# Attention and maxout FFN on one core: twin PSUM tiles in the prologue, other slots for the steps, and 30 of 40 transposes moved from TensorE to the DMA crossbar

## Chip, cores, metric

The kernel runs on one core of a Trainium2 chip. The metric is the device time of one execution in microseconds; lower is better. A "fast" run is one within 1.5% of the fastest run of the same kernel, and verdicts use fast runs alone.

## The reference

Eight batches of eight heads, 576 tokens, head size 64. Keys and values are averaged over groups of eight tokens, so attention goes over 72 pooled positions. The result, 4608 tokens by 512, passes through a maxout FFN.

```python
k_p = k.reshape(B, H, Sp, 8, D).mean(axis=3)         # Sp = 72
v_p = v.reshape(B, H, Sp, 8, D).mean(axis=3)
attn = softmax(q @ k_p.transpose / sqrt(D))
x = (attn @ v_p).transpose(0, 2, 1, 3).reshape(B * S, H * D)
h = maximum(maximum(x @ w1, x @ w2), x @ w3)         # 512 -> 768
out = h @ w_out                                      # 768 -> 512
```

## The kernel before

The FFN works in nine blocks of 512 tokens, and the attention of the next batch (576 tokens) is cut into steps that are emitted in chosen "slots" between the FFN's parts. The parts that matter here:

```python
def turn_x(b, c0, keep, xn, tag):          # 128 tokens of attention output, turned to [channel, token]
    pxt = psp.tile([128, KCH, 128], F16, name="pxt", ...)
    for kc in range(KCH):                  # KCH = 4
        nc.tensor.transpose(pxt[:, kc, :], xn[...], identh)
    nc.scalar.copy(out=xT[:, :, g0 + keep:g0 + 128], in_=pxt[:, :, keep:128])

def values(b, c0):                         # 8 matmuls into pav, then on DVE:
    ...
    xn = sb3.tile([128, 2, 4, D], F16, name="xn", tag="xn")     # sb3: three buffers
    nc.vector.tensor_tensor(out=xn, in0=pv[:, :, :, 0:D], in1=rcp..., op=ALU.mult)

CHUNKS = ((0, 0), (128, 0), (256, 0), (384, 0), (448, 64))      # five turns per batch

def hidden_part(n, jc, c0, c1, hT):        # three weights: 4 matmuls each on xT, ACT cast, DVE max, DVE max
    ...
def project(n, hT):
    for mm in range(4):
        # 6 matmuls into po
        osb = sb3.tile([128, C], F32, name="osb", tag="osb", bufs=5)
        nc.scalar.copy(out=osb, in_=po)
        for u in range(2):
            nc.sync.dma_start(out=dst[...], in_=osb[64 * u:64 * u + 64, :])    # 128 KB each
        yield

for n in range(1, TOK // NB):
    if n + 2 < B:
        fold_k(n + 2, nc.gpsimd); load_k(n + 3, nc.gpsimd)      # 1152 KB
        fold_v(n + 2); load_v(n + 3, nc.gpsimd); load_q(n + 3)  # 1152 and 576 KB
    # (the loads only where n + 3 < B)
    nxt = batch(n + 1)
    for part in (hidden(n, hT), project(n, hT)):
        for _ in part:
            # next(nxt) as often as PLAN names this slot
```

PE is TensorE, DVE is VectorE, ACT is ScalarE and POOL is GpSimd. `xn` is one chunk of attention output (128 tokens in rows), `xT` the input of the FFN with channels in rows; bringing the one into the other is called a turn. `et` are the exponentials, `kz` the keys as the scores need them, `pw`, `po` and the other p-names are tiles in PSUM. The landing of a transfer is counted from its issue.

The softmax here doesn't subtract the row's maximum and nothing guards it: scores larger than these inputs give would overflow.

Of the kernel before, what the change touches and what calls it, by code (L numbers as in the profile page):

```python
# [14 lines left out]
def kernel(  # L15
# [11 lines left out]
    nc = tc.nc  # L27
    dt = mybir.dt
    F32, BF16, F16 = dt.float32, dt.bfloat16, dt.float16

    B, H, S, D = q.shape
    POOL = 8
    Sp = S // POOL
# [12 lines left out]
    JCH = DFF // 128  # L46
# [8 lines left out]
    psp = ctx.enter_context(tc.tile_pool(name="psp", bufs=1, space=PSUM))  # L55
    ctx.enter_context(tc.manual_schedule())

    kts, vts, qbs, kps, qTs, ets = {}, {}, {}, {}, {}, {}
# [45 lines left out]
    identh = const.tile([128, 128], F16, name="identh", tag="identh")  # L104
# [39 lines left out]
    def pool_v(b, h, g, tag, evac):  # L144

        pvp = psp.tile([128, g - h, D], F32, name="pvp", tag=tag[0], bufs=tag[1])
        for j in range(POOL):
            nc.tensor.matmul(pvp, identh[0:Sp, :], vts[b][:, h:g, j, :],  # L148
                             start=(j == 0), stop=(j == POOL - 1))
        evac(out=vp_all[:, b, h:g, 0:D], in_=pvp[0:Sp])  # L150

    def turn_q(b, n0, n1, evac, tag):
        if b not in qTs:
            qTs[b] = sb2.tile([128, 2 * NG, 128], BF16, name="qT", tag="qT")
        pqt = psp.tile([128, n1 - n0, 128], BF16, name="pqt", tag=tag[0],
                       bufs=tag[1])
        qf = qbs[b].rearrange("p hp t d -> p (hp t d)")
        for n in range(n0, n1):
            nc.tensor.transpose(pqt[:, n - n0, :], qf[:, 128 * n:128 * n + 128],  # L159
                                ident)  # L160
        evac(out=qTs[b][:, n0:n1, :], in_=pqt)  # L161

    def turn_k(b, evacs, tag):
        pkt = psp.tile([128, 6, 96], BF16, name="pkt", tag=tag[0], bufs=tag[1])
        for i in range(6):
            nc.tensor.transpose(pkt[:, i, :], kps[b][:, i, :, :], ident[0:96, 0:96])
        for par in range(2):
            rows = slice(64 * par, 64 * par + 64)
            evacs[par](  # L169
                out=kz_all[b % 2][rows, par, :, 0:Sp].rearrange(  # L170
                    "p h (r i) -> p h r i", i=6),
                in_=pkt[rows].rearrange("p i (h r) -> p h r i", h=H))

    def pool_k(b, tag):

# [26 lines left out]
        score(b, h, psc[:, 512:576], 1, 3, 4)  # L202
        exp(ets[b][:, h, :], psc[0:Sp, 0:S])

    def turn_x(b, c0, keep, xn, tag):
        pxt = psp.tile([128, KCH, 128], F16, name="pxt", tag=tag[0], bufs=tag[1])
        for kc in range(KCH):
            nc.tensor.transpose(  # L208
                pxt[:, kc, :],
                xn[:, kc // 2, 2 * (kc % 2):2 * (kc % 2) + 2, :], identh)  # L210
        g0 = S * b + c0
        nc.scalar.copy(out=xT[:, :, g0 + keep:g0 + 128], in_=pxt[:, :, keep:128])  # L212

    def values(b, c0):
        pav = psp.tile([128, 2, 512], F32, name="pav", tag="att", bufs=2)
# [14 lines left out]
    CHUNKS = ((0, 0), (128, 0), (256, 0), (384, 0), (448, 64))  # L230
    TR = ("tr", 1)
    PW = ("pw", 3)
    V_V = (nc.vector.tensor_copy, nc.vector.tensor_copy)

    def queries(b):

        new_et(b)
        for m, (n0, n1) in enumerate(((0, 5), (5, 10), (10, 14), (14, 18))):
            turn_q(b, n0, n1, nc.scalar.copy, TR)
            yield  # L240
            if m == 2 and b > 1:
                turn_k(b, V_V, TR)
                yield
        for h in range(H):
            scores(b, h)
            yield

    def outputs(b, tags=(TR,) * 5):

        last = None  # L250
        for (c0, keep), tag in zip(CHUNKS, tags):
            xn = values(b, c0)
            yield
            if last:
                turn_x(*last)
                yield
            last = (b, c0, keep, xn, tag)
        turn_x(*last)
        yield
# [22 lines left out]
    def hidden(n, hT):  # L282

        halves = n < 2
        if halves:
            for c0 in (0, NB // 2):
                for jc in range(2):
                    yield from hidden_part(n, jc, c0, c0 + NB // 2, hT)
        for jc in range(2 if halves else 0, JCH):
            yield from hidden_part(n, jc, 0, NB, hT)  # L290

    def project(n, hT):
# [15 lines left out]
    def new_hT():  # L308
        return sb2.tile([128, JCH, NB], F16, name="hT", tag="hT")
# [4 lines left out]
    def heat(n):  # L314
        for _ in range(n):
            nc.tensor.matmul(wm, warm[:, 0:128], warm, start=True, stop=True)  # L316

    new_et(0)
    heat(14)
    new_kp(0)  # L320
    k16 = const.tile([96, 6, 4, D], F16, name="k16", tag="k16")
    pkp0 = psp.tile([128, 6, D], F32, name="pkp", tag="pw", bufs=3)

    def spread(i0, i1):
        nc.vector.tensor_copy(out=kps[0][:, i0:i1, 0, :], in_=pkp0[0:96, i0:i1])
        nc.scalar.copy(out=kps[0][:, i0:i1, 1, :], in_=pkp0[0:96, i0:i1])

    for i in (0, 2, 4):
        c = slice(i, i + 2)
        nc.vector.tensor_tensor(out=k16[:, c], in0=kts[0][:, c, 0:4],  # L330
                                in1=kts[0][:, c, 4:8], op=ALU.add)
        for j in range(4):
            nc.tensor.matmul(pkp0[:, c], identh[0:96, :], k16[:, c, j, :],
                             start=(j == 0), stop=(j == 3))
        if i == 2:
            spread(0, 4)
        else:
            heat(1)
    spread(4, 6)
    heat(2)  # L340
    turn_k(0, (nc.vector.tensor_copy, nc.scalar.copy), PW)
    turn_q(0, 0, 5, nc.scalar.copy, PW)
    turn_q(0, 5, 9, nc.vector.tensor_copy, PW)

    def scores4(h):
        psc = psp.tile([128, 4, 256], F32, name="psc4", tag="att", bufs=2)
        for i in range(4):
            score(0, h + i, psc[:, i, :], 0, 0, 4)
        exp(ets[0][:, h:h + 4, 0:256], psc[0:Sp])

    def scores2(h):
        psc = psp.tile([128, 2, 512], F32, name="psc2", tag="att", bufs=2)
        for i in range(2):
            score(0, h + i, psc[:, i, 0:64], 0, 4, 5)
            score(0, h + i, psc[:, i, 64:320], 1, 0, 4)
        exp(ets[0][:, h:h + 2, 256:S], psc[0:Sp, :, 0:320])

    scores4(0)
    turn_q(0, 9, 14, nc.vector.tensor_copy, PW)
    turn_q(0, 14, 18, nc.vector.tensor_copy, PW)  # L360
    heat(1)
    scores4(4)
    scores2(0)
    pool_v(0, 0, 4, PW, nc.vector.tensor_copy)
    scores2(2)
    pool_v(0, 4, 6, PW, nc.vector.tensor_copy)
    scores2(4)
    pool_v(0, 6, 8, PW, nc.vector.tensor_copy)
    scores2(6)
    out0 = outputs(0, (PW, PW, TR, TR, TR))  # L370
    next(out0)
    heat(1)
    next(out0)
    heat(2)
    next(out0)
    heat(2)
    next(out0)
    next(out0)


    nc.vector.memset(kz_all[1], 0.0)
    hT0 = new_hT()
    def early():
        pool_k(1, TR)
        yield
        turn_k(1, V_V, TR)
        yield
        yield from queries(1)

    side = early()  # L390
    steps = {16: 1, 17: 1, 19: 1, 20: 1, 21: 1, 22: 1, 23: 2}
    for slot, _ in enumerate(hidden(0, hT0)):
        if slot < 5:
            next(out0, None)
        for _ in range(steps.get(slot, 0)):
            next(side)
    next(side)
    pool_v(1, 0, 4, TR, nc.scalar.copy)
    next(side)
    next(side)  # L400
    pool_v(1, 4, 8, TR, nc.scalar.copy)
    for _ in side:
        pass
    side = outputs(1)
    for _ in project(0, hT0):
        next(side)
        next(side)
    fold_k(2, nc.gpsimd)
    load_k(3, nc.gpsimd)
    load_q(3)  # L410
# [4 lines left out]
    def batch(b):  # L415
# [1 line left out]
        yield from outputs(b)  # L417


    PLAN = (1, 2, 4, 5, 7, 8, 9, 10, 11, 12, 13, 14, 15, 16, 17, 17, 18, 18, 19, 19,  # L420
            20, 20, 21)
    PLAN1 = (7, 8, 10, 13, 14, 15, 16, 17, 18, 19, 20, 21, 22, 23, 24, 24, 25, 25, 26,
             26, 27, 27, 27)
    for n in range(1, TOK // NB):
        if n + 2 < B:
            fold_k(n + 2, nc.gpsimd)
            if n + 3 < B:
                load_k(n + 3, nc.gpsimd)
            fold_v(n + 2)
            if n + 3 < B:  # L430
                load_v(n + 3, nc.gpsimd)
                load_q(n + 3)
        hT = new_hT()
        nxt = batch(n + 1) if n + 1 < B else iter(())
        plan = PLAN1 if n == 1 else PLAN
        slot = 0
        for part in (hidden(n, hT), project(n, hT)):
            for _ in part:
                if slot in (0, 2):
                    next(side, None)  # L440
                for _ in range(plan.count(slot)):
                    next(nxt, None)
                slot += 1
        for _ in nxt:
            pass


# [28 lines left out]
```

## Time and profile before

| | |
|---|---|
| time, median of 4 runs | 269.28 us |
| TensorE busy | 250.4 of 267.3 us (94%) |
| first FFN matmul | 20.83 us |
| first FFN matmul of block 2 | 84.21 us |
| a block with attention beside it / without | 27.36 / 20.72 us |

The prediction shows the busy table, the chain and TensorE's timeline. Two more rows: the granted TensorE clock and the busy share of the DMA engines, each in tenths for 40 slices of the span, and the line of DMA packets.

```profile
PEclk9999999999999999999999999999999999999998
DMA  7999999698757958969777604200330033006006
...
DMA packets 20866, 34.71 MB, mean 130 GB/s; under 512 B 2636, under 2 KB 13260, under 8 KB 20268
```

The clock is full throughout. The DMA engines are half busy or more until about 150 us, mostly with loads for later batches. TensorE waits for none of them.

### The profile page before, as it was taken

The page shows a single profiled execution, that of the slowest core. Times are in us where ns is not written, and L with a number is a line of the kernel's source. Part 1 is how long each engine was busy: PE and PEld are TensorE (multiplying, and loading weights), DVE is VectorE, ACT ScalarE, POOL GpSimd, SP SyncE. Part 2 cuts the span into 40 slices and gives each one's busy share as a digit, 9 for nine tenths or more (in the row PEclk, how much of TensorE's full clock was granted, in tenths as well). Part 3 has the DMA queues.
Part 4 walks back from the last instruction along what each step waited for, and adds up shares of the span by engine and source line. Part 5 has one row for each costly group of instructions (what it writes and reads, how often), then busy time and mean ns, then how long its engine had stood idle before and what let it go on. Part 6 is the DMA issues. An engine that isn't in the chain of part 4 may idle for free.

```text
span 267.3 us, 4638 instructions
## 1 busy us (share of the span) xinstructions
PE 250.4 (94%) x1858; PEld 139.6 (52%) x1860; DVE 128.1 (48%) x227; ACT 132.9 (50%) x232; POOL 117.7 (44%) x84
## 2 busy tenths in 40 slices
PE   7598998998998999999999999999999999999993
PEld 2477546574555455545555555545554554444441
DVE  3447562555453646363645464455536464433440
ACT  1374248553755474547465655465555653223221
POOL 8662002999899999859970895000000000000000
PEclk9999999999999999999999999999999999999998
DMA  7999999698757958969777604200330033006006
GB/s 188 201 198 205 202 244 211 168 245 180 178 121 180 285 126 184 256 202 174 178 156 221 94 0 105 54 0 2 85 76 0 0 81 79 0 22 139 0 2 156
DMA packets 20866, 34.71 MB, mean 130 GB/s; under 512 B 2636, under 2 KB 13260, under 8 KB 20268
## 3 DMA queue, kind: packets, MB, share of 16 engines
q0 software_dynamic: 14048, 21.44, 41.1%
q1 hardware_dynamic: 6796, 12.98, 19.3%
q8 instruction: 14, 0.23, 0.4%
q14 instruction: 8, 0.07, 0.1%
HBM read 34.60 MB, written 9.44 MB: 165 GB/s over the span
## 4 chain that ended last, share of the span: by engine, by line
PE 83%; DVE 9%; ACT 5%; issue 1%; DVEq 0%; ACTq 0%
PE pw L267 45%; PE po L297 17%; PE psc L188 6%; PE pxt L208 4%; PE pqt L159 3%; DVE kz L169 3%; PE pav L217 3%; PE wm L316 3%; ACT et L193 2%; DVE xn L225 2%; DVE t L275 2%; ACT t L272 1%; PE pvp L148 1%; DVE hT L278 1%; ACT qT L161 1%
## 5 line engine op out<-in xcount | busy, mean ns | idle before, releaser
L267 PE MATMUL pw<-xT,mw 128*128 128x512 f16 (+1 forms) x696 | 157.2, 364 | 0.9 <-ACT xT L212 0.7
L267 PEld LDWEIGHTS <-mw 128*128 128x128 f16 x696 | 62.2, 98 | 50.9 <-issue 1.2
L275 DVE TENSOR_TENSOR t<-t,pw 128x512 f16<-128x512 f16 (+1 forms) x58 | 37.8, 651 | 79.0 <-PE pw L267 48.4
L272 ACT CAST t<-pw 128x512 f16<-128x512 f32 (+1 forms) x58 | 32.3, 557 | 43.2 <-PE pw L267 42.6
L297 PE MATMUL po<-mwo,hT 128*128 128x512 f16 x216 | 51.5, 379 | 0.0
L193 ACT ACTIVATE et<-psc 72x576 f16<-72x576 f32 (+2 forms) x62 | 40.5, 662 | 13.0 <-PE psc L188 12.9
L278 DVE TENSOR_TENSOR hT<-t,pw 128x512 f16<-128x512 f16 (+1 forms) x58 | 37.7, 650 | 15.4 <-PE pw L267 13.4
L127 POOL TENSOR_TENSOR vt<-vt 72x2048 f32<-72x2048 f32 (+1 forms) x12 | 41.2, 3434 | 2.6 <-DMA vt<-in_v_dram 2.1
L127 POOL TENSOR_TENSOR kt<-kt 96x1536 f32<-96x1536 f32 (+1 forms) x12 | 31.5, 2624 | 22.7 <-DMA kt<-in_k_dram 22.1
L301 ACT COPY osb<-po 128x512 f32<-128x512 f32 x36 | 21.1, 586 | 30.5 <-PE po L297 30.5
L297 PEld LDWEIGHTS <-hT 128*128 128x128 f16 x216 | 19.8, 98 | 18.9 <-DVE hT L278 0.4
L212 ACT COPY xT<-pxt 128x512 f16<-128x512 f16 (+1 forms) x40 | 21.8, 545 | 14.3 <-PE pxt L208 14.3
L225 DVE TENSOR_TENSOR xn<-pav,rcp 128x512 f16<-128x512 f32 x40 | 27.7, 692 | 1.4
L188 PE MATMUL psc<-qT,kz 128*128 128x64 bf16 (+3 forms) x192 | 25.4, 246 | 3.1 <-ACT qT L161 1.7
L161 ACT COPY qT<-pqt 128x640 bf16<-128x640 bf16 (+1 forms) x29 | 18.6, 641 | 18.1 <-PE pqt L159 18.1
L188 PEld LDWEIGHTS <-kz 128*128 128x128 bf16 x192 | 18.1, 98 | 17.5 <-issue 2.9
L217 PEld LDWEIGHTS <-et 72*128 72x128 f16 x320 | 15.7, 98 | 8.2 <-issue 0.6
L223 DVE RECIPROCAL rcp<-pav 128x8 f32<-128x8 f32 x40 | 8.1, 204 | 23.1 <-PE pav L217 23.1
L208 PE MATMUL pxt<-identh,xn 128*128 128x128 f16 x160 | 15.5, 219 | 2.3 <-DVE xn L225 2.1
L217 PE MATMUL pav<-vp,et 72*128 72x65 f16 x320 | 17.1, 194 | 0.4 <-ACT et L193 0.3
L159 PEld LDWEIGHTS <-qb 128*128 128x128 bf16 x144 | 9.9, 97 | 11.4 <-DVE kz L169 5.3
L159 PE MATMUL pqt<-ident,qb 128*128 128x128 bf16 x144 | 13.0, 219 | 2.7 <-DVE kz L169 2.3
(41 smaller groups left out, 107.9 us busy)
## 6 DMA issues: line engine op xcount, KB each, us to landing
out_dram<-osb SPq DMA_DIRECT2D x72, 128.0 KB, 2.4
kt<-in_k_dram POOLq DMA_DIRECT2D x5, 1152.0 KB, 7.6
vt<-in_v_dram POOLq DMA_DIRECT2D x5, 1152.0 KB, 10.2
qb<-in_q_dram POOLq DMA_DIRECT2D x7, 576.0 KB, 11.8
mw<-in_moe_w_dram POOLq DMA_DIRECT2D x9, 256.0 KB, 9.7
kt<-in_k_dram SPq DMA_DIRECT2D x3, 384.0 KB, 5.1
kt<-in_k_dram SPq DMA_DIRECT2D x1, 1152.0 KB, 9.5
vt<-in_v_dram SPq DMA_DIRECT2D x1, 1152.0 KB
```

The source lines that it names most:

```text
L127: e.tensor_tensor(out=t[:, :, 0:n, :], in0=t[:, :, 0:n, :], in1=t[:, :, n:2 * n, :], op=ALU.add)
L159: nc.tensor.transpose(pqt[:, n - n0, :], qf[:, 128 * n:128 * n + 128], ident)
L188: nc.tensor.matmul(out, kz_all[b % 2][:, f % 2, h, :], qTs[b][:, n + i0:n + i1, 64 * (h % 2):64 * (h % 2) + 64], start=True, stop=True)
L193: nc.scalar.activation(out=out, in_=in_, func=FT.Exp, scale=1.0 / 64.0)
L208: nc.tensor.transpose(pxt[:, kc, :], xn[:, kc // 2, 2 * (kc % 2):2 * (kc % 2) + 2, :], identh)
L217: nc.tensor.matmul(pav[:, h // 4, 65 * (h % 4):65 * (h % 4) + 65], ets[b][:, h, c0:c0 + 128], vp_all[:, b, h, :], start=True, stop=True)
L225: nc.vector.tensor_tensor(out=xn, in0=pv[:, :, :, 0:D], in1=rcp.to_broadcast([128, 2, 4, D]), op=ALU.mult)
L267: nc.tensor.matmul(pw, w_sb[wi][:, kc, bass.ts(jc, 128)], xT[:, kc, col], start=(kc == 0), stop=(kc == KCH - 1))
L272: nc.scalar.copy(out=t, in_=pw)
L275: nc.vector.tensor_tensor(out=t1, in0=t, in1=pw, op=ALU.max)
L278: nc.vector.tensor_tensor(out=hT[:, jc, c0:c1], in0=t, in1=pw, op=ALU.max)
L297: nc.tensor.matmul(po, hT[:, jc, bass.ts(mm, 128)], wo_sb[:, jc, :], start=(jc == 0), stop=(jc == JCH - 1))
```

## The change

The intent is to take work off TensorE, the bound. In the prologue, two copies of a PSUM tile let DVE and ACT read at once, and the first chunks' values come earlier. Steps move to other slots, and the first two blocks work in half blocks for longer. For batches 2 to 7 the turn of the attention output becomes a DMA transpose on the sync queue, from xn in SBUF straight to xT, without PSUM and without the ACT copy.

```diff
+    def turn_x(b, c0, keep, xn, tag, evac=nc.scalar.copy):
+        if b > 1:
+            g0 = S * b + c0
+            nc.sync.dma_start_transpose(
+                out=xT[:, :, g0 + keep:g0 + 128],
+                in_=xn.rearrange("p g h d -> p (g h d)")[keep:128])
+            return
...
-    pkp0 = psp.tile([128, 6, D], F32, name="pkp", tag="pw", bufs=3)
+    pkp0 = [psp.tile([128, 6, D], F32, name="pkp", tag="pw", bufs=3)
+            for _ in range(2)]
...
+    pkt0 = [keys(0, PW) for _ in range(2)]
+    for h in (0, 4):
+        fill_kz(0, 0, h, h + 4, pkt0[0], nc.vector.tensor_copy)
+        fill_kz(0, 1, h, h + 4, pkt0[1], nc.scalar.copy)
...
-                for jc in range(2):
+                for jc in range(3):
...
-    PLAN = (1, 2, 4, 5, 7, 8, 9, 10, 11, 12, 13, 14, 15, 16, 17, 17, 18, 18, 19, 19,
-            20, 20, 21)
+    PLAN = (2, 4, 5, 6, 8, 8, 9, 10, 11, 12, 13, 14, 15, 16, 17, 18, 18, 19, 19, 20,
+            20, 21)
...
-        for _ in nxt:
-            pass
+        side = nxt
```

(Cut: the order of the prologue, the slots of batch 1, PLAN1.)

More of the change, by code (lines that the diff above doesn't have):

```diff
@@ L161, in turn_q, with keys @@
         evac(out=qTs[b][:, n0:n1, :], in_=pqt)
-    def turn_k(b, evacs, tag):
+    def keys(b, tag):
         pkt = psp.tile([128, 6, 96], BF16, name="pkt", tag=tag[0], bufs=tag[1])
@@ L166, in turn_k, with fill_kz @@
             nc.tensor.transpose(pkt[:, i, :], kps[b][:, i, :, :], ident[0:96, 0:96])
-        for par in range(2):
-            rows = slice(64 * par, 64 * par + 64)
-            evacs[par](
-                out=kz_all[b % 2][rows, par, :, 0:Sp].rearrange(
-                    "p h (r i) -> p h r i", i=6),
-                in_=pkt[rows].rearrange("p i (h r) -> p h r i", h=H))
+        return pkt
+    def fill_kz(b, par, h0, h1, pkt, evac):
+        rows = slice(64 * par, 64 * par + 64)
+        evac(out=kz_all[b % 2][rows, par, h0:h1, 0:Sp].rearrange(
+                 "p h (r i) -> p h r i", i=6),
+             in_=pkt[rows, :, 12 * h0:12 * h1].rearrange("p i (h r) -> p h r i", r=12))
+    def turn_k(b):
+        pkt = keys(b, TR)
+        for par in range(2):
+            fill_kz(b, par, 0, H, pkt, nc.vector.tensor_copy)
     def pool_k(b, tag):
@@ L203, in scores @@
         exp(ets[b][:, h, :], psc[0:Sp, 0:S])
-    def turn_x(b, c0, keep, xn, tag):
+    def turn_x(b, c0, keep, xn, tag, evac=nc.scalar.copy):
[5 more added lines that the diff above has]
+            return
         pxt = psp.tile([128, KCH, 128], F16, name="pxt", tag=tag[0], bufs=tag[1])
@@ L211, in turn_x @@
         g0 = S * b + c0
-        nc.scalar.copy(out=xT[:, :, g0 + keep:g0 + 128], in_=pxt[:, :, keep:128])
+        evac(out=xT[:, :, g0 + keep:g0 + 128], in_=pxt[:, :, keep:128])
     def values(b, c0):
@@ L232 @@
     PW = ("pw", 3)
-    V_V = (nc.vector.tensor_copy, nc.vector.tensor_copy)
     def queries(b):
@@ L240, in queries @@
             yield
-            if m == 2 and b > 1:
-                turn_k(b, V_V, TR)
+            if m == (3 if b == 2 else 2) and b > 1:
+                turn_k(b)
                 yield
@@ L286, in hidden @@
             for c0 in (0, NB // 2):
-                for jc in range(2):
+                for jc in range(3):
                     yield from hidden_part(n, jc, c0, c0 + NB // 2, hT)
-        for jc in range(2 if halves else 0, JCH):
+        for jc in range(3 if halves else 0, JCH):
             yield from hidden_part(n, jc, 0, NB, hT)
@@ L318 @@
     new_et(0)
-    heat(14)
+    ATT = ("att", 2)
     new_kp(0)
     k16 = const.tile([96, 6, 4, D], F16, name="k16", tag="k16")
-    pkp0 = psp.tile([128, 6, D], F32, name="pkp", tag="pw", bufs=3)
-    def spread(i0, i1):
-        nc.vector.tensor_copy(out=kps[0][:, i0:i1, 0, :], in_=pkp0[0:96, i0:i1])
-        nc.scalar.copy(out=kps[0][:, i0:i1, 1, :], in_=pkp0[0:96, i0:i1])
+    pkp0 = [psp.tile([128, 6, D], F32, name="pkp", tag="pw", bufs=3)
+            for _ in range(2)]
+    heat(16)
     for i in (0, 2, 4):
@@ L331 @@
                                 in1=kts[0][:, c, 4:8], op=ALU.add)
-        for j in range(4):
-            nc.tensor.matmul(pkp0[:, c], identh[0:96, :], k16[:, c, j, :],
-                             start=(j == 0), stop=(j == 3))
-        if i == 2:
-            spread(0, 4)
-        else:
+        for p in pkp0:
+            for j in range(4):
+                nc.tensor.matmul(p[:, c], identh[0:96, :], k16[:, c, j, :],
+                                 start=(j == 0), stop=(j == 3))
+        if i > 0:
+            c = slice(i - 2 if i == 2 else i, i + 2)
+            nc.vector.tensor_copy(out=kps[0][:, c, 0, :], in_=pkp0[0][0:96, c])
+            nc.scalar.copy(out=kps[0][:, c, 1, :], in_=pkp0[1][0:96, c])
+        if i < 4:
             heat(1)
-    spread(4, 6)
-    heat(2)
-    turn_k(0, (nc.vector.tensor_copy, nc.scalar.copy), PW)
     turn_q(0, 0, 5, nc.scalar.copy, PW)
-    turn_q(0, 5, 9, nc.vector.tensor_copy, PW)
+    turn_q(0, 5, 9, nc.vector.tensor_copy, ATT)
+    pkt0 = [keys(0, PW) for _ in range(2)]
+    for h in (0, 4):
+        fill_kz(0, 0, h, h + 4, pkt0[0], nc.vector.tensor_copy)
+        fill_kz(0, 1, h, h + 4, pkt0[1], nc.scalar.copy)
+    heat(1)
     def scores4(h):
@@ L359, with rest @@
     turn_q(0, 9, 14, nc.vector.tensor_copy, PW)
-    turn_q(0, 14, 18, nc.vector.tensor_copy, PW)
+    turn_q(0, 14, 18, nc.scalar.copy, PW)
+    pool_v(0, 0, 4, PW, nc.vector.tensor_copy)
+    scores4(4)
+    pool_v(0, 4, 6, PW, nc.vector.tensor_copy)
+    pool_v(0, 6, 8, PW, nc.vector.tensor_copy)
+    scores2(0)
+    xn0 = [values(0, c0) for c0, _ in CHUNKS[:2]]
     heat(1)
-    scores4(4)
-    scores2(0)
-    pool_v(0, 0, 4, PW, nc.vector.tensor_copy)
+    turn_x(0, 0, 0, xn0[0], PW)
     scores2(2)
-    pool_v(0, 4, 6, PW, nc.vector.tensor_copy)
+    heat(1)
+    turn_x(0, 128, 0, xn0[1], PW, nc.vector.tensor_copy)
     scores2(4)
-    pool_v(0, 6, 8, PW, nc.vector.tensor_copy)
+    heat(1)
     scores2(6)
-    out0 = outputs(0, (PW, PW, TR, TR, TR))
-    next(out0)
-    heat(1)
-    next(out0)
-    heat(2)
-    next(out0)
-    heat(2)
-    next(out0)
-    next(out0)
+    def rest():
+        for c0, keep in CHUNKS[2:]:
+            xn0.append(values(0, c0))
+            yield
+            if c0 > 256:
+                turn_x(0, last, 0, xn0[-2], TR)
+                yield
+            last = c0
+        turn_x(0, last, keep, xn0[-1], TR)
+        yield
     nc.vector.memset(kz_all[1], 0.0)
     hT0 = new_hT()
+    out0 = rest()
     def early():
@@ L385, in early @@
         yield
-        turn_k(1, V_V, TR)
+        turn_k(1)
         yield
@@ L390 @@
     side = early()
-    steps = {16: 1, 17: 1, 19: 1, 20: 1, 21: 1, 22: 1, 23: 2}
+    steps = {19: 1, 20: 1, 21: 1, 22: 1, 23: 1, 24: 2, 25: 2, 26: 2}
     for slot, _ in enumerate(hidden(0, hT0)):
-        if slot < 5:
+        if slot > 0:
             next(out0, None)
@@ L396 @@
             next(side)
-    next(side)
-    pool_v(1, 0, 4, TR, nc.scalar.copy)
-    next(side)
-    next(side)
-    pool_v(1, 4, 8, TR, nc.scalar.copy)
-    for _ in side:
-        pass
-    side = outputs(1)
-    for _ in project(0, hT0):
-        next(side)
-        next(side)
+    out1 = outputs(1)
+    for mm, _ in enumerate(project(0, hT0)):
+        if mm == 0:
+            pool_v(1, 0, 4, TR, nc.scalar.copy)
+            next(side)
+            pool_v(1, 4, 8, PW, nc.vector.tensor_copy)
+        next(side, None)
+        if mm > 0:
+            next(out1)
+        if mm > 1:
+            next(out1)
+    side = out1
     fold_k(2, nc.gpsimd)
@@ L417, in batch @@
         yield from outputs(b)
-    PLAN = (1, 2, 4, 5, 7, 8, 9, 10, 11, 12, 13, 14, 15, 16, 17, 17, 18, 18, 19, 19,
-            20, 20, 21)
-    PLAN1 = (7, 8, 10, 13, 14, 15, 16, 17, 18, 19, 20, 21, 22, 23, 24, 24, 25, 25, 26,
-             26, 27, 27, 27)
+    PLAN = (2, 4, 5, 6, 8, 8, 9, 10, 11, 12, 13, 14, 15, 16, 17, 18, 18, 19, 19, 20,
+            20, 21)
+    PLAN1 = (9, 11, 13, 15, 18, 19, 20, 21, 22, 23, 24, 25, 26, 26, 27, 27, 28, 28, 29,
+             29, 30, 30)
     for n in range(1, TOK // NB):
@@ L438 @@
             for _ in part:
-                if slot in (0, 2):
+                if slot < 8:
                     next(side, None)
@@ L443 @@
                 slot += 1
-        for _ in nxt:
-            pass
+        side = nxt
 _INS = ['q', 'k', 'v', 'moe_w1', 'moe_w2', 'moe_w3', 'moe_w_out']
```

## The prediction

> **What bounds the kernel now.** I read the page's busy table first, then the chain that ended last, then the TensorE timeline of one steady block, and last the stores on the sync queue.
>
> ```profile
> PE 250.4 (94%) x1858; PEld 139.6 (52%) x1860; DVE 128.1 (48%) x227; ACT 132.9 (50%) x232; POOL 117.7 (44%) x84
> ...
> PE 83%; DVE 9%; ACT 5%; issue 1%; DVEq 0%; ACTq 0%
> PE pw L267 45%; PE po L297 17%; PE psc L188 6%; PE pxt L208 4%; PE pqt L159 3%; DVE kz L169 3%; PE pav L217 3%; PE wm L316 3%; ACT et L193 2%; DVE xn L225 2%; DVE t L275 2%; ACT t L272 1%; PE pvp L148 1%; DVE hT L278 1%; ACT qT L161 1%
> ```
>
> TensorE is busy 94% of 267.3 us and carries 83% of the chain; no other engine passes 50%. So only time taken off TensorE, or idle time of TensorE, counts. The 30 removed ACT copies (about 0.59 us each) save nothing by themselves. The timeline of TensorE at the end of one steady block and the start of the next (start, length, work; the length contains the drain, so what a group costs is the distance to the next start):
>
> ```profile
> 131.83 0.40 PE L208 MATMUL pxt<-identh,xn 128*128 128x128 f16 x4 [0.25 <-DVE xn L225]
> 132.06 1.46 PE L297 MATMUL po<-mwo,hT 128*128 128x512 f16 x6
> 133.36 0.42 PE L217 MATMUL pav<-vp,et 72*128 72x65 f16 x8
> 133.62 0.39 PE L208 MATMUL pxt<-identh,xn 128*128 128x128 f16 x4
> 133.84 1.46 PE L297 MATMUL po<-mwo,hT 128*128 128x512 f16 x6
> ```
>
> Four transposes start at 133.62 and the projection follows at 133.84: a chunk's turn costs 0.22 us, not 0.39. A projection of 128 tokens costs 1.30 us and the values of one chunk 0.26. The table of stretches gives 27.36 us for such a block with attention beside it and 20.72 for one without.
>
> The stores of the results go through the sync queue, and so will the new transposes. The view of the output tensor, then that queue over one projection phase:
>
> ```profile
> L305 SPq DMA_DIRECT2D out_dram<-osb x72: 466/594/1826, 49.0 to 263.8; - x72
> ...
> DMA to landing us min/median/max: 2.2/2.4/8.7
> ```
> ```profile
> 161.52 6.46 SPq L305 DMA_DIRECT2D out_dram<-osb  x8
> ```
>
> A 128 KB store keeps the queue's engine 0.47 to 0.59 us, two of them about 1.1 us per projection tile. It lands 2.2 to 2.4 us later on a quiet machine, up to 8.7 us when loads are in flight: by small windows 6 to 8 us around 80 to 84 and 107 to 111 us, 2.3 to 3 around 163.
>
> **What the skill says.** [...]"VectorE: DVE Perf Modes", The three transpose paths, gives 1309 ns for one 128x128 by the DMA crossbar against 390 on TensorE; no transfer of this kind is in the trace before, and one chunk here is four such squares. "DMA: Bandwidth & Descriptors", Queues, rings and completion order, says that each DMA engine alternates between queues by whole packets. The trace agrees: the stores are slow just when key loads with 12 KB packets share the engines with their 2 KB ones. "PSUM — Partial Sum Buffer", PSUM bank collisions raise a hardware error, says that two engines may not touch one bank and quadrant together; in the trace ACT waits 1.13 us until DVE has read the same tile, which is what the twin tiles attack.
>
> **The change part by part.**
>
> (a) Prologue. The first real FFN matmul starts at 20.83 us. Today kz is filled by DVE (9.99, 0.75 us), then by ACT (10.77, 0.63), then ACT copies qT until 12.12, and scores start at 12.17. With two tiles and half fills the query copies go first, while the keys (12 transposes at 55 ns, twice as many) run. I estimate DVE's first half from 10.4 and ACT's from 10.7, each about 0.4 us, so scores at about 11.1: one microsecond gained. Two chunks' values now follow the third exp instead of the sixth; ACT's five exps today run from 14.38 to 18.08 ahead of them. But ACT now has a query copy too, and the xn chain (0.21 + 0.69 us each, then turn and copy) stays. I put the first FFN matmul at 19.0 to 19.5: **gain 1.5 us**.
>
> (b) Block 0 (20.83 to 54.04). TensorE idles here about 2.3 us, most of it twice 0.5 us at batch 1's scores and at pkp/pkt. Spreading the scores over later slots keeps much of this; batch 1's second chunk is now turned just before block 1 needs it, which costs its ACT copy (0.6 us). **Gain 0.5 us**.
>
> (c) Block 1 (54.04 to 84.21). Idle before kz 1.16, before xn 0.80, two smaller of 0.34 and 0.24: 2.5 us, of which I take 1.9. Batch 2's five turns go: 5 x 0.22 = 1.1. **Gain 3.0 us**.
>
> (d) Blocks 2 to 6. Each loses five turns (1.1), the 0.25 idle at xn and the 0.23 at kz in front of the last query turn, since the key turn moves one slot: 1.58 us, times five **7.9 us**.
>
> Sum of gains: 1.5 + 0.5 + 3.0 + 7.9 = **12.9 us**.
>
> (e) What it adds. A block n+1 starts with a matmul that needs 512 columns of xT. Batch n+1 starts at 576(n+1), so the block needs its first 512 - 64(n+1) tokens: 384 and 320 for blocks 2 and 3 (three chunks), 256 and 192 for 4 and 5 (two), 128 and 64 for 6 and 7 (one). The plan puts turns 0, 1, 2, 3 behind projection tiles 0, 1, 2, 3, and in the sync queue each stands behind that tile's two stores. Take T as the end of tile 0's projection; tiles then end every 1.30 + 0.26 = 1.56 us and the next block could start at T + 4.68. A store starts about 0.8 us after its tile (134.17 against 133.36). Let a transpose hold the queue 0.6 us and land 2.4 us after its issue (both estimates, from the stores of equal size). Then stores 0 take T+0.8 to 1.9, turn 0 starts at 1.9 and lands 4.3; stores 1 2.5 to 3.6, turn 1 lands 6.0; stores 2 4.2 to 5.3, turn 2 lands 7.7. Blocks 2 and 3 wait 7.7 - 4.68 = 3.0 us each, blocks 4 and 5 6.0 - 4.68 = 1.3 each, 6 and 7 nothing. **Loss 2 x 3.0 + 2 x 1.3 = 8.6 us.**
>
> DVE also waits: xn has three buffers, so the fourth chunk's xn waits for turn 0's landing (T+4.3), the fifth for turn 1's. The next block's first maximum comes at T+6.5 or later, so this hardly reaches TensorE.
>
> Net: 269.3 - 12.9 + 8.6 = **265.0 us**.
>
> **The rivals.**
> 1. The crossbar is hidden: landing near 2.0 us and little queue time. Then turn 2 lands at about 7.1 and turn 1 at 5.5: the loss is 2 x 2.4 + 2 x 0.8 = 6.4 us; with a better prologue about 261. For it: someone placed the slots with care, and chose even batch 2 for the DMA. Against it: program order in the sync queue behind stores that cannot start before ACT has copied.
> 2. The sync queue becomes the bound of the projection phase. Holding it 1.2 us per turn makes 2.3 us of work per 1.56 us tile: turn 1 is issued at 4.2 and lands near 7, turn 2 at 6.5 and lands near 9.4, a loss of 2 x 4.7 + 2 x 2.3 = 14 us and 270.4 us. For it: 1309 ns for a quarter of a chunk. Against it: one wide transfer need not cost four times a small one.
> 3. Loads in flight stretch the landing at the ends of blocks 1 and 2, as they did the stores: up to 5 us more for each of two blocks, 270 or above. For it: the DMA row of the page stands at 7 to 9 tenths until 150 us. Against it: at 76 to 80 us, where block 1 will now end, the engines are quiet in this trace.
> 4. Long stalls let TensorE's clock drop. The granted clock is 1.00 in nearly all stretches, but no stall there is longer than about 1.3 us; a drop would add a few microseconds.
>
> **Range and chances.** Gains are good to about 2.5 us, the new waits lie between 5.5 and 14. That spans 261 to 270; I widen it a little to 259.5 to 270.5. Faster by over 2% means below 264.0, just under the middle. The slots look chosen with measurements in hand, which pulls down a little: 0.45 faster, 0.48 within 2%, 0.07 slower. I put the point at 264.8.
>
> **What would show it.** Right: TensorE idle before the first matmul of blocks 2 to 5, released by DMA xT, near 3 us twice and 1.3 us twice, and none at 6 and 7; the middle of a steady block 1.5 us shorter; the first FFN matmul near 19.2 us; ACT busy about 16 us less. The sync queue's rows give the held time and the landing of a transpose, 0.6 and 2.4 by my estimate. Wrong: no wait on xT at all (rival 1 and more), waits at every block and on xn too (rival 2), waits only at blocks 2 and 3 (rival 3), or a granted clock well under 1.

## The result and the profile after

The changed kernel takes 322.13 us (319.95 to 322.72, 4 runs), against 269.28 us. The ratio is 1.195 (95% interval 1.189 to 1.201). Ratios here are the mean time of one kernel's fast runs over that of the other's in the same rounds, so not quite the ratio of the medians.

The page after: busy table, clock and DMA rows, packets, and the head of the chain.

```profile
PE 252.5 (79%) x1780; PEld 137.2 (43%) x1780; DVE 128.5 (40%) x233; ACT 117.9 (37%) x204; POOL 117.6 (37%) x84
...
PEclk9999999999855579995799956999999999999999
DMA  8999997876998925589045792316402601714105
...
DMA packets 35649, 38.25 MB, mean 119 GB/s; under 512 B 17420, under 2 KB 28044, under 8 KB 35052
...
PE 67%; DMA 12%; issue 10%; ACT 4%; DVE 3%; SPq 2%; DVEq 0%; ACTq 0%
```

TensorE's busy time is about what it was, but its share fell to 79%. The clock row has three holes at 5 tenths. There are some 14,800 packets more, and the sizes under 512 B account for them: a transpose of 128 KB travels in 256 B pieces.

TensorE's timeline shows where the time lies. These are the first FFN matmuls of blocks 2 to 5, with the idle time ahead of them in brackets, and the first of block 6, which had none:

```profile
110.86 5.20 PE L278 MATMUL pw<-xT,mw 128*128 128x512 f16 x12 [29.21 <-issue]
151.46 5.28 PE L278 MATMUL pw<-xT,mw 128*128 128x512 f16 x12 [12.52 <-DMA xT<-xn]
192.05 5.28 PE L278 MATMUL pw<-xT,mw 128*128 128x512 f16 x12 [12.03 <-issue]
222.76 2.76 PE L278 MATMUL pw<-xT,mw 128*128 128x512 f16 x12 [2.28 <-DMA xT<-xn]
...
248.31 2.75 PE L278 MATMUL pw<-xT,mw 128*128 128x512 f16 x12
```

TensorE stands still for 29.2, 12.5, 12.0 and 2.3 us. After the three long waits the same twelve matmuls take 5.2 to 5.3 us instead of 2.76: the clock has dropped to half (0.50 to 0.52 granted in these stretches, 0.99 to 1.00 after them). Two waits are put down to "issue", meaning that the profile found no releaser. For the one before block 2 the landing below settles whose it is; for the one before block 4 the views give no landing of the turn that it needed last. The view of xT gives the time that a transpose holds the sync queue (shortest, median, longest), and the time from issue to landing:

```profile
L214 SPq DMA_TRANSPOSE xT<-xn x30: 1172/1254/7037, 78.7 to 280.5; - x30
...
DMA to landing us min/median/max: 2.3/2.9/25.4
```

The sync queue at the end of block 1:

```profile
81.36 1.24 SPq L214 DMA_TRANSPOSE xT<-xn  x1
82.69 2.55 SPq L316 DMA_DIRECT2D out_dram<-osb  x2
85.34 1.23 SPq L214 DMA_TRANSPOSE xT<-xn  x1
```

The transpose issued at 85.34 is batch 2's third turn, the last that block 2 needs. A narrow window of the DMA view gives its landing as 25.4 us after issue, at 110.7; block 2 starts at 110.86. The one at 81.36 took 12.6 us, and the same batch's first, at 78.67, took 2.5.

The difference adds up on the profiled spans (320.8 and 267.3 us, 53.5 apart). TensorE was free for block 2 at 81.65 against 84.21 before, which is 2.6 gained; an undisturbed block is 25.55 us long (222.76 to 248.31) against 27.36, which gains 1.81 in each of five, 9.1. Lost are the waits of 56.3 us in all (a last one of 0.24, for DVE, included). The three blocks that ran partly at half clock took 28.1 to 28.6 us of TensorE time instead of 25.55, 8.4 together, of which 7.5 is in the first twelve matmuls. 56.3 + 8.4 - 2.6 - 9.1 = 53.0.

So the gains were nearly as forecast, and the landing of the transposes turned the result. Three questions remain. Is it the loads, the sync queue, or the crossbar? Why so slow? And is the crossbar worth anything?

### The profile page after: what moved, and what is told of

Read it like the earlier page. It is cut to its first block, busy times and chain, and to the rows that moved or that the text cites. A ratio compares the mean times of both kernels' runs of the same rounds, so it can differ in the third digit from the quotient of the medians.

```text
span 320.8 us, 4564 instructions
## 1 busy us (share of the span) xinstructions
PE 252.5 (79%) x1780; PEld 137.2 (43%) x1780; DVE 128.5 (40%) x233; ACT 117.9 (37%) x204; POOL 117.6 (37%) x84
## 4 chain that ended last, share of the span: by engine, by line
PE 67%; DMA 12%; issue 10%; ACT 4%; DVE 3%; SPq 2%; DVEq 0%; ACTq 0%
PE pw L278 43%; DMA xT<-xn 12%; PE po L308 9%; PE psc L194 5%; PE pqt L159 3%; PE pav L229 2%; PE wm L327 2%; SPq L316 2%; ACT et L199 1%; PE pvp L148 1%; DVE kz L171 1%; ACT osb L312 1%; PE pxt L220 1%; ACT xT L224 1%; PE pkt L166 1%
## 5 line engine op out<-in xcount | busy, mean ns | idle before, releaser
L278 PE MATMUL pw<-xT,mw 128*128 128x512 f16 (+1 forms) x720 | 165.0, 370 | 57.0 <-issue 41.2
L278 PEld LDWEIGHTS <-mw 128*128 128x128 f16 x720 | 66.0, 100 | 113.2 <-issue 52.2
L237 DVE TENSOR_TENSOR xn<-pav,rcp 128x512 f16<-128x512 f32 x40 | 27.7, 692 | 53.8 <-DMA xT<-xn 52.8
L86 POOL DMA_DIRECT2D qb<-in_q_dram x9 | 7.0, 776 | 71.5 <-PE psc L194 69.1
L161 ACT COPY qT<-pqt 128x640 bf16<-128x640 bf16 (+1 forms) x30 | 19.2, 639 | 28.6 <-PE pqt L159 28.6
L194 PE MATMUL psc<-qT,kz 128*128 128x64 bf16 (+3 forms) x192 | 26.2, 246 | 0.8 <-DVE kz L171 0.5
L171 DVE COPY kz<-pkt 64x576 bf16<-64x576 bf16 (+1 forms) x16 | 11.4, 716 | 4.4 <-PE pkt L166 4.2
```

Source lines behind the costliest of these rows:

```text
L194: nc.tensor.matmul(out, kz_all[b % 2][:, f % 2, h, :], qTs[b][:, n + i0:n + i1, 64 * (h % 2):64 * (h % 2) + 64], start=True, stop=True)
L278: nc.tensor.matmul(pw, w_sb[wi][:, kc, bass.ts(jc, 128)], xT[:, kc, col], start=(kc == 0), stop=(kc == KCH - 1))
```

## The experiments

Twelve kernels ran, on three chips of the same kind; each was timed against the kernel before on its own chip (median 269.2 to 269.4 us).

### 1. Every turn back on TensorE

```diff
-        if b > 1:
+        if b > B:
             g0 = S * b + c0
             nc.sync.dma_start_transpose(
```

> The changed kernel with every turn back on TensorE; prologue, slots and halves stay changed. Theory (the transfers are the whole loss, the rest of the change is a gain): no wait of TensorE on a DMA of xT, granted clock near 1.00, first FFN matmul at 18.7 us as in the changed kernel, 262 to 267 us. Rival (the moved slots cost something as well): over 270 us.

Measured: 264.48 us (264.30 to 264.85), ratio 0.982 (0.981 to 0.984), correct. Nothing waits on a DMA of xT, and the clock is at 9 tenths in all but the last slice. The rest of the change is worth 4.7 us. All of the loss, and more, belongs to the 30 transfers.

### 2. No loads in flight

```diff
-                load_k(n + 3, nc.gpsimd)
+                kts[n + 3] = kts[n + 1]
```

and the same for values and queries, so batches 4 to 7 are computed from old tiles and the result is wrong.

> Wrong result on purpose: the changed kernel, but the key, value and query loads of batches 4 to 7 are not made and old tiles are used again; crossbar turns, stores and their order stay. Theory (the loads in flight starve the crossbar transposes): each lands 2.3 to 2.5 us after issue as in the undisturbed blocks, the waits before blocks 2 and 3 shrink from 29 and 12.5 us to about 5 us, those before 4 and 5 to about 2.4 us, the clock stays near 1.00, 268 to 276 us in all. Rival (the sync queue, held 1.25 us by each transpose and sharing with the stores, is the cause): still over 300 us.

Measured: 279.30 us (278.78 to 280.08), ratio 1.038. TensorE's timeline and the landings:

```profile
86.58 5.28 PE L278 MATMUL pw<-xT,mw 128*128 128x512 f16 x12 [5.02 <-issue]
119.87 4.04 PE L278 MATMUL pw<-xT,mw 128*128 128x512 f16 x12 [5.10 <-DMA xT<-xn]
149.41 4.44 PE L278 MATMUL pw<-xT,mw 128*128 128x512 f16 x12 [2.31 <-issue]
179.02 2.76 PE L278 MATMUL pw<-xT,mw 128*128 128x512 f16 x12 [2.29 <-DMA xT<-xn]
```
```profile
DMA to landing us min/median/max: 2.3/2.4/4.2
```

The waits are the expected ones to a tenth, and the long landings are gone. The total is 3 us over my range, because I had counted on a full clock: even these waits were followed by slow stretches in three of four cases (4.04 to 5.28 us for twelve matmuls). The loads account for 43 of the 53 us; what is left of the waits, 14.7 us, is another cause.

### 3. A plain copy in place of the crossbar

```diff
-            nc.sync.dma_start_transpose(
+            nc.sync.dma_start(
                 out=xT[:, :, g0 + keep:g0 + 128],
-                in_=xn.rearrange("p g h d -> p (g h d)")[keep:128])
+                in_=xn.rearrange("p g h d -> p (g h d)")[
+                    :, 0:4 * (128 - keep)].rearrange("p (k t) -> p k t", k=KCH))
```

Wrong result: the same bytes, queue and place, without the turn. (The last chunk of a batch goes in 128 B pieces.)

> Wrong result on purpose: each crossbar transpose is replaced by a plain copy from xn to the same place in xT, on the same queue, of the same bytes in the same number of pieces (512 of 256 B); all loads stay. Theory a (a transfer of many small packets loses against loads with 4 and 12 KB packets, whatever it does): landings of 10 to 25 us and over 310 us. Theory b (the crossbar transpose alone suffers so): landings under load of 3 to 9 us, as the stores of the kernel before had, the wait before block 2 under 12 us, 270 to 290 us.

Measured: 301.06 us in its one fast run; the three others, 306.1 to 308.0, are over 1.5% above it and count as slow, and so does the profiled one. So there is no interval, but every run lies more than 11% above the kernel before. The copies' times in the sync queue and to landing:

```profile
L214 SPq DMA_DIRECT2D xT<-xn x30: 637/650/1442, 77.8 to 263.4; - x30
...
DMA to landing us min/median/max: 2.1/2.3/16.4
```

Neither theory is quite met. A plain copy of the same small pieces also lands up to 16.4 us late, and in the profiled run blocks 2, 3 and 4 wait 17.8, 12.4 and 11.0 us, the last two about as long as with the crossbar. So most of the harm is not the crossbar's own. But it stays below the crossbar's 25.4 us, 29.2 us and 322 us; part of that may be the held queue (0.65 us a copy against 1.25 us a transpose), which this run does not separate. The packet records of the kept traces show one thing that comes with the crossbar: after 74 us, 49 packets of the changed kernel, of turns, loads and stores alike, each took over 2 us (10.9 at most). With the plain copy no packet did, and in the three kernels with every turn on TensorE (before, experiments 1 and 7) there was one in all, of 2.04 us. Nor did any without loads (experiment 2) or with held loads (experiment 5), so it takes both. Why they stand still stays open.

### 4. Which load, and does packet size decide?

Without the value loads alone (`vts[n + 3] = vts[n + 1]`), wrong:

> Wrong result on purpose: the changed kernel without the value loads of batches 4 to 7 (72 rows, packets of 4 KB); key and query loads stay. In the changed kernel the fewest 256 B packets went by (12 to 69 in 2 us) beside value loads, more (57 to 248) beside key loads. Theory (the value loads do most of it): the waits before blocks 2 to 4 fall under 10 us each, 280 to 295 us. Rival (the key loads with their 12 KB packets do most of it): over 305 us.

Without the key loads alone (`kts[n + 3] = kts[n + 1]`); the comparison passes all the same, although these keys are wrong, so correctness says nothing here:

> Wrong result on purpose: the changed kernel without the key loads of batches 4 to 7 (96 rows, packets of 12 KB); value and query loads stay. Theory (the value loads do most of it): waits of over 10 us stay before blocks 2 to 4, over 300 us. Rival (the key loads do most of it): 280 to 295 us.

With both loads converted to 16 bit on their way, which was meant to give small packets (`load_k(n + 3, nc.gpsimd, F16)`, likewise for values):

> Correct: the changed kernel, with the key and value loads of batches 3 to 7 converted to 16 bit on their way, so that their packets are 512 to 1024 B instead of 12 and 4 KB; the turns and the timing of the issues stay. Theory (the engines take turns packet by packet, so it is the size of the load's packets that makes a 512-packet transfer slow): turns land within 8 us beside these loads, 275 to 295 us. Rival (any load in flight holds the small packets up, whatever its packet size): landings of 10 to 25 us, over 310 us.

| kernel | time, us | ratio | longest landing, us | waits before blocks 2, 3, 4, us |
|---|---|---|---|---|
| changed | 322.13 | 1.195 | 25.4 | 29.2, 12.5, 12.0 |
| no key loads | 295.65 | 1.099 | 12.9 | 13.2, 10.8, 5.2 |
| no value loads | 287.23 | 1.068 | 7.5 | 9.7, 6.3, 4.3 |
| 16 bit on their way | 303.79 | 1.122 | 14.4 | 17.3, 9.2, 8.3 |
| none of k, v, q | 279.30 | 1.038 | 4.2 | 5.0, 5.1, 2.3 |

The value loads cost more than the key loads, but each costs much. Without value loads time and waits are as expected. Without key loads I had expected over 300 us and waits over 10 us before all three blocks; two of the three are, and the time is 295.65. Packet size stays undecided. With 16 bit the landings got shorter, but stayed over the 8 us that I expected. But the edit did not do what I had written: the trace shows value packets of 1024 B, and key packets of 6144 B, so only halved; query packets stayed at 1152 B. That run is also not clean in time: GpSimd folds 16 bit data faster, so the value load of batch 4 starts at 77.0 us instead of 80.6, ahead of the turns. Counting the trace's packets by size in windows of 2 us in the changed kernel (stores left out) shows that they don't go one for one:

```
window, us   in flight beside the turns     load packets     256 B packets of turns
 84 to  86   values                         101 of 4096 B     12
 90 to  92   queries                        218 of 1152 B    166
 98 to 100   keys                            17 of 12288 B    57
218 to 220   no load                          0              512 (one whole turn)
```

Beside queries it is nearly one for one, beside keys three small ones for each large, beside values one for eight. The row beside keys is no fair share, though: in that window 12.0 of the 16.6 packets in flight on average are such as took over 1 us, key packets (0.46 us at that window's median) and stores. What sets these numbers stays open. That a load in flight delays the turns does not.

### 5. The same loads at another time

The loads for batches 4 to 7 start behind the fifth FFN part of the block that folds them, and are nearly over when its first turn is issued (the last query load lands at 109.8 and 144.6 us, the first turns are issued at 110.6 and 144.5). Same bytes, same packets, right result.

```diff
+                if slot == 5 and 2 <= n < B - 2:
+                    after((load_k(n + 2, nc.gpsimd),), mark[0])   # waits for that part's last matmul
+                    load_v(n + 2, nc.gpsimd)
+                    load_q(n + 2)
+                    fold_k(n + 2, nc.gpsimd)
+                    fold_v(n + 2)
```

(and out of the head of the loop, where only batch 3's folds stay)

> Correct: the changed kernel, but the loads for batches 4 to 7 are started behind the fifth FFN part of the block that folds them, so that they land before its projection phase, where the crossbar turns run. Same bytes, same packets, same turns. Theory (loads in flight at the same time are the cause, not the loads as such): landings of 2.3 to 3 us for the turns that the next block needs, waits of about 5, 5, 2.3 and 2.3 us before blocks 2 to 5 as without loads, 276 to 283 us. Rival (the loads cost TensorE by another way, such as late data): over 290 us.

Measured: 279.36 us (278.80 to 279.65), ratio 1.035. The starts of blocks 2 to 5:

```profile
85.71 1.44 PE L280 MATMUL pw<-xT,mw 128*128 128x512 f16 x3 [4.72 <-issue]
118.51 1.44 PE L280 MATMUL pw<-xT,mw 128*128 128x512 f16 x3 [5.10 <-DMA xT<-xn]
149.62 0.81 PE L280 MATMUL pw<-xT,mw 128*128 128x512 f16 x3 [2.44 <-issue]
177.55 0.82 PE L280 MATMUL pw<-xT,mw 128*128 128x512 f16 x3 [2.29 <-DMA xT<-xn]
```

The waits are as in experiment 2, and the total is the one without any loads (279.30, on another chip). The turns that a block waits for land in 2.4 to 2.5 us. A later turn, which meets the next block's loads, takes up to 9.5 us, and no block waits for it. So it is not the loads but their being in flight together with the turns.

### 6. Turns ahead of the stores

What remains is the order in the sync queue. Each turn stands behind two stores that cannot start before ACT has copied their tile. Here turns come one slot earlier, and the stores of a tile are issued behind that slot's steps:

```diff
             nc.scalar.copy(out=osb, in_=po)
+            yield
             for u in range(2):
                 ...
                 nc.sync.dma_start(out=dst[:, GS[g], :], in_=osb[64 * u:64 * u + 64, :])
-            yield
```

with PLAN's last ten steps at 16, 17, 17, 18, 18, 19, 19, 20, 20, 21, and PLAN1 one slot earlier throughout. First with held loads:

> Correct: as the kernel with held loads, and each turn is put one slot earlier and ahead of the stores of its projection tile in the sync queue, since a store cannot start before ACT has copied its tile. Theory (what is left without loads is the order in the sync queue, not the 2.4 us of landing): the third turn is issued about 2 us and lands about 4.4 us after the first projection tile, before the 4.7 us at which the next block starts: no wait on xT over 0.5 us, 255 to 260 us, under the kernel with every turn on TensorE (264.5). Rival (the landing itself is too long): waits of over 2 us stay before blocks 2 and 3, over 264 us.

Measured: 258.53 us (258.24 to 258.76), ratio 0.958 (0.955 to 0.962), correct. This beats both kernels. The starts of blocks 2 and 3, the only ones that still wait on xT, and the page's clock row:

```profile
81.61 0.82 PE L280 MATMUL pw<-xT,mw 128*128 128x512 f16 x3 [0.41 <-DMA xT<-xn]
108.19 0.81 PE L280 MATMUL pw<-xT,mw 128*128 128x512 f16 x3 [0.94 <-DMA xT<-xn]
```
```profile
PEclk9999999999999999999999999999999999999999
```

One wait is 0.94 us where I expected none over 0.5. Then the order alone, with the loads where the change has them:

> Correct: the changed kernel with only the order in the sync queue changed (turns one slot earlier and ahead of the stores), loads where they were. With the two kernels with held loads this makes a square of two by two. Theory (both causes are there, the loads the larger): order alone takes off what it took off with held loads, about 20 us, or a little more where a turn now gets in ahead of a load, but turns that meet loads still land after 8 us or more: 285 to 305 us. Rival (with the turns early enough, the loads do no harm): under 265 us.

Measured: 272.0 to 283.5 us in four runs, median 276.8; only the fastest counts as fast. In the profiled run, one of the slow ones, the waits are 13.0, 2.4 and 1.4 us. That is less than I expected: there the turns that blocks 3 and 4 need get through ahead of a load (batch 3's third turn lands in 2.9 us, its fourth takes 13.1). The one of batch 2 still meets the loads and takes 13.0 us. Without held loads the time scatters by 11 us; that this hangs on which transfer comes first is likely, but not shown. Turns issued from another queue than the stores' would be another way to the same order; that was not run.

| | stores ahead (as changed) | turns ahead |
|---|---|---|
| loads as changed | 322.1 | 272.0 (the one fast run; four runs up to 283.5) |
| loads held | 279.4 | 258.5 |

### 7. What the crossbar is worth once hidden

The kernel of 258.5 us with its turns back on TensorE (the edit of experiment 1):

> Correct: the fastest kernel so far (held loads, turns ahead of the stores, 258.5 us) with its turns of batches 2 to 7 on TensorE again. It measures what the crossbar itself is worth once its transfers are hidden. By the prediction's own figure (30 turns of 0.22 us, 6.6 us, and some short waits on xn): 264 to 267 us. Rival (held loads and order did the work, not the crossbar): 258 to 260 us.

Measured: 266.07 us (265.89 to 266.52), ratio 0.988. The crossbar takes 7.5 us off (258.53, on another chip). Held loads and order do nothing good for a kernel that turns on TensorE: without them it took 264.48 us, 1.6 us less. Against that best kernel with turns on TensorE the crossbar gains 6.0 us.

### 8. The crossbar for the last two batches only

No loads are in flight there, so this should be a plain gain:

```diff
-        if b > 1:
+        if b > 5:
```

> The changed kernel with the crossbar for batches 6 and 7 only, TensorE for 2 to 5. Theory (without loads in flight, and where one chunk alone is needed at once, the crossbar is a plain gain): no wait on xT, each of these two batches saves five turns of 0.22 us and a wait, so 2 to 3 us under the kernel with every turn on TensorE, about 260 to 264 us. Rival (the crossbar costs as much by the held queue as it saves): within 1 us of it.

Measured: 264.29 us (263.73 to 264.40), so the same as with every turn on TensorE (264.48, same chip): a miss. Against the kernel before the ratio is 0.981, which the 2% rule leaves unclear. DVE's and TensorE's timelines in block 6:

```profile
188.54 0.69 DVE L237 TENSOR_TENSOR xn<-pav,rcp 128x512 f16<-128x512 f32 x1 [2.38 <-DMA xT<-xn]
192.85 0.69 DVE L237 TENSOR_TENSOR xn<-pav,rcp 128x512 f16<-128x512 f32 x1 [3.51 <-DMA xT<-xn]
193.46 0.68 DVE L286 TENSOR_TENSOR t<-t,pw 128x512 f16<-128x512 f16 x1
```
```profile
194.19 1.02 PE L278 MATMUL pw<-xT,mw 128*128 128x512 f16 x4 [1.69 <-DVE t L286]
```

xn has three buffers, and a transpose keeps one until it has landed. DVE, in order, waits to write the fifth chunk's xn until 192.85, does its maximum late, and TensorE waits 1.69 us for a PSUM tile. With six buffers (`tag="xn", bufs=6`):

> Correct: crossbar for batches 6 and 7 only, and six buffers for xn instead of three. With three, DVE waited up to 3.5 us for a transfer to release xn, and TensorE 1.69 us for DVE in block 6. Theory (that wait ate the gain of these two batches): no wait of DVE on a DMA of xT and none of TensorE over 0.5 us, 261 to 263 us. Rival (the gain of a removed turn is smaller than 0.22 us times five): 264 us as with three buffers.

Measured: 261.63 us (261.31 to 262.29), ratio 0.970. No wait of DVE or TensorE on a transfer is left, and the kernel is 2.9 us under the one with every turn on TensorE (measured on another chip, where the kernel before took 269.42 against 269.19 us). Six buffers without the crossbar were not run, so that they do nothing by themselves is not shown.

## Why the prediction was wrong

The record said 264.8 us, 259.5 to 270.5; measured were 322.13. By its steps:

- **Part (e), what the change adds: the step that failed.** "Let a transpose hold the queue 0.6 us and land 2.4 us after its issue." The landing is right without loads (2.4 to 2.7 us for the turns that a block waits for in experiment 2). The hold is 1.25 us, twice the estimate. It came from stores of equal size, and a plain copy of the same pieces does take 0.65; the crossbar does not. And beside loads the turns that blocks 2 and 3 waited for last took 25.4 and 8.5 us to land. Instead of 8.6 us the four waits were 56.0: 14.7 as without loads, which is the longer hold and the order in the queue, and 41.3 more beside the loads.
- **Rival 3 had the mechanism, with its size wrong.** It allowed "up to 5 us more for each of two blocks". It was 24 us more before block 2 and 7 to 10 before blocks 3 and 4 (against experiment 2). I had scaled from the stores, which go as 2 KB packets and took 8.7 us at most in the kernel before; in experiment 3 plain copies in 256 B pieces took up to 16.4 us, and the transposes 25.4. The argument against it, that the engines were quiet at 76 to 80 us, held for just one turn: the value load started at 80.6 us. I had also misread which loads slow the stores. The prediction names key loads with 12 KB packets alone; but the stores issued at 80 to 82 us of the trace before took 5.6 to 8.2 us to land, and between 77 and 90 us no 12 KB packet started: in flight were a value load with 4 KB packets and a query load.
- **Rival 2 was right for the part without loads.** It said a hold of 1.2 us, landings at T+7 and T+9.4, waits of 4.7 twice and 2.3 twice, 14 us. Experiment 2 has 5.0, 5.1, 2.3 and 2.3, 14.7 us. That it fits so closely is partly luck. The second and third turn were issued at T+4.7 and T+7.3 (81.15 and 83.77 us, T at 76.47), later than its 4.2 and 6.5, and landed sooner after their issue, 2.5 and 2.7 us against the 2.8 and 2.9 that its numbers imply.
- **Rival 4 came true as well.** The long waits cost about 8 us more at half clock (8.4 in the sum above). I said "a few microseconds".
- **"This hardly reaches TensorE" was wrong** where nothing else waited. In experiment 8, DVE's wait for xn's buffer cost 1.69 us at one place and, with all that hung on it, 2.7 us in all. In the changed kernel DVE waits 52.8 us on these transfers, but mostly in the shadow of TensorE's own wait: TensorE's FFN matmuls wait only 0.2 us for DVE.
- **Gains (a) to (d), 12.9 us, were nearly right in sum, 11.7, but partly by luck.** (a) The prologue brought 2.2 (18.68 against 20.83 us), more than the 1.5, though the scores start at 11.61 us, only 0.56 earlier instead of one microsecond. The rule on one bank and quadrant, as the prediction quotes it, does not explain ACT's wait of 1.13 us: the two fills of kz read rows 0 to 63 and 64 to 127 of the tile, which have no row in common. The trace shows that ACT waited, and that with two tiles the fills overlap (DVE from 11.11 us, ACT from 11.29), but not why the wait was there. (b) Block 0 failed: it grew from 33.21 to 34.17 us (18.68 to 52.85) instead of losing 0.5. It waits 0.84 us for kz at 35.14, 0.75 for the exponentials at 48.41 and 0.67 for xT before block 1. (c) Block 1 became 1.4 us shorter (30.17 to 28.80), not 3.0: of its waits those for kz (0.48 us) and for the exponentials (0.51) are in new places. (d) A steady block gains 1.81 us, a little over 1.58.
- **The evidence that was given the wrong weight** is the slots "chosen with measurements in hand". I let it pull the chances down to 0.07 for slower, with two rivals of my own at 270 us or above. The trace spoke for them, and nothing in it for the trust.

## What to carry to other kernels

A transfer that takes the place of compute inherits everything else on its queue and its engines. Before moving work to the DMA, list what else is in flight in that window, and move prefetches out of it; a prefetch that nobody waits for can still hold up what somebody does. Then put the latency-bound transfer ahead of the stores in its queue, and give its source enough buffers for its landing time: here the same 30 transposes, against turns on TensorE (264.5 us), made the kernel 22% slower or 2.3% faster.

## What the Trainium skill lacked or had wrong

- "DMA: Bandwidth & Descriptors", Rules for kernel authors, says that a transpose next to ordinary DMAs needs nothing. For the result that held in every correct kernel here. For the time it did not: a median of 2.4 us to landing without loads in flight (4.2 at most), up to 25.4 us beside loads, with 49 packets that took over 2 us each.
- The same page, Queues, rings and completion order, has each engine alternate between queues by packets. The counts here were 101 packets of 4096 B to 12 of 256 B beside value loads, 218 to 166 beside query loads, and 17 to 57 beside key loads. A packet there is a group of descriptors; whether the trace's packets are the same thing no run shows, so these counts do not refute the page. But it has nothing from which they follow.
- "Advanced Engine Details and Errata", X-Bar Transpose (TRN2), calls transposes as fast as regular DMAs. Landing undisturbed is (median 2.4 us without loads; a copy of the same pieces 2.3). The time that one holds the issuing queue is not: 1.25 against 0.65 us for 128x512, and this section gives none.
- "VectorE: DVE Perf Modes", The three transpose paths, gives 1309 ns for 128x128 by the crossbar without saying what of it is queue and what is landing. A 128x512 here: 1.25 us and a median of 2.4 us.
- "TensorE: Matmul & The Clock Gate", Why this matters for your kernels, warns of idle gaps over about 3 us. Experiment 2 has a wait of 2.31 us that was followed by twelve matmuls in 4.44 us (granted clock 0.60), and one of 2.29 us that was followed by the same twelve in 2.76 (1.00).
